# A convolution kernel whose GpSimd pieces and VectorE sums are put in another order, and whose pieces are held behind an earlier VectorE instruction

## The chip, the cores and the metric

The kernel runs on one core of a Trainium2 chip. The core's engines are TensorE (PE, matrix products; its weight loads are listed as PEld), VectorE (DVE), ScalarE (ACT), GpSimd (POOL) and SyncE (SP, which here only issues DMAs). Each engine works through its own queue in order, and engines wait for each other on semaphores. The metric is the device time of one execution in microseconds (us): the median of three runs of the kernel before is 270.39 us (270.06 to 271.07).

## The reference

A gated causal convolution over time with three taps, two steps apart, followed by a projection:

```python
B, T, D, K, dil = 2, 16000, 256, 3, 2
h = sum over i of  xp[:, pad - 2*i : pad - 2*i + T] @ w[i]     # w[i]: 256 x 512, pad = 4
f, g = h[..., :D], h[..., D:]
z = tanh(f) * sigmoid(g)
return z @ w_o                                                  # w_o: 256 x 256
```

Inputs and the output are bf16.

## The kernel before

**Fast convolution.** Time steps are laid out as rows of J neighbouring steps (`xt`, transposed on load, 128 channels on the partitions). For J = 4 (a B group) four products of 512 columns, each in two contraction steps, give two pairs of output steps in place of six products; for J = 6 (an A group) five products give three pairs. The price is linear combinations of the input ("input sums") ahead of the products, and linear combinations of the results behind them.

**Input sums.** For a B group: `m`, `p`, `d0`, `d3`. For an A group: `u0`, `u1`, `u2`, `e`, `f`, three scalings of `u1` (`u3`, `uh`, `ud`), and four sums on top of others: `rp` = f + u1 and `rm` = e + u3, made by an accumulating DMA that POOL issues, and `r0` = u0 + uh and `ri` = u2 + ud. Sums of 128x1024 elements are VectorE's (`pre`, L434 for two inputs, L432 for a scaling). `r0`, `ri` and, from group 5 on, `d0` and `d3` are GpSimd's, each in four quarters of 128x256, called pieces. Sixteen pieces `wa` (L351) build a weight for the A groups at the start. The trace names `r0` by the tile `u`, `d0` and `d3` by `d`.

**Blocks and slots.** There are 12 A groups and 13 B groups with four blocks each (one 128-wide part of the 512 outputs), 100 blocks in all: first 16 B blocks, then A and B mixed 48 to 28, then 8 B blocks. The main loop takes one block per turn `k`, called slot k here. In slot k TensorE makes the "first" product of block k (and "mid" for an A block), "last" of block k - 1, "zero" and "inf" of block k - 2 (`product`, L453), and one or two output pieces of the projection (`out_mm`, L565). So `m` or `u1` is due in a group's first slot, `p` and `rp` one later, `d0`, `d3`, `r0` and `ri` two later, `rm` in the first slot's "mid". ScalarE copies the first product out (`ss`), applies tanh and sigmoid, and evicts the projection.

**VectorE's order in a slot.** A gate (tanh times sigmoid, L547; 128x1024 for B, 128x1536 for A, every other slot of a group, and for one small remainder `zo`, L543), then a *combine* (L487, reading PSUM) of block k - 1, a second one for an A block, and `halfway` (L487) for block k if that is an A block. All L487 operations are called combines here; they are the only ones that read PSUM. Between them stand the input sums, at *stops*: each gate and each first combine calls `at_stop`, which takes the next line of the string `PLAN`. Of a line "`a > b ; c`", `b` are sums that VectorE makes at this stop, `c` pieces and DMAs that go to POOL's queue, and `a` are sums made at the end of the slot (`ahead`).

**Holds.** A piece is issued with a wait (`hold`) for an earlier VectorE instruction, the `latest` one that `note` has recorded: the last sum of the stop, or, without sums, the gate or combine before it. So pieces start when the stop's combine starts. The two kinds of DMA have no such wait; POOL issues them in its order once their inputs are there.

```python
def at_stop():
    sums(stop[1])
    gpsimd(stop[2])
    stop = next(stops, [[], [], []])
```

**Loads.** SP issues the transposing load of a group (L286) at the end of the slot 15 ahead of its `wanted` slot; an A or a B group's tile has four buffers.

Of the kernel before, what the change touches and what calls it, by code (L numbers as in the profile page):

```python
# [117 lines left out]
>uh.9;ri.9
>u3.9 p.9;r0.9 d3.9 d3.9
>f.9;  # L120
>;rm.9 d0.9
# [16 lines left out]
>f.11;d3.10
>u2.11;rp.11 d3.10 d3.10
>uh.11;  # L140
>;rm.11 d3.11 d0.11
>ud.11 u0.11;r0.11 d3.11 ri.11 d3.12
>;ri.11 d0.12 r0.11 r0.11 ri.11
# [33 lines left out]
def kernel(  # L177
# [10 lines left out]
    nc = tc.nc  # L188
# [3 lines left out]
    K, _, D2 = w.shape  # L192
# [148 lines left out]
    def weights_a(n):  # L341

        if n < 2 * K:
            tap, ct = n % K, n // K
            nc.scalar.mul(wu_sb[tap][ct][:], w_taps[tap][:, ct, :], (-2.0 / 3.0, -1.0 / 3.0, -1.0 / 6.0)[tap])
            return None
        n -= 2 * K
        add, ct, part = n // (2 * W_A), n // W_A % 2, n % W_A
        d = slice(part * D2 // W_A // 16 * 16, (part + 1) * D2 // W_A // 16 * 16)
        dst = (wu_sb[0][ct], wa_sb[:, ct, :])[add]  # L350
        return nc.gpsimd.tensor_tensor(out=dst[:, d], in0=wu_sb[0][ct][:, d], in1=wu_sb[1 + add][ct][:, d], op=ALU.add)  # L351
# [65 lines left out]
    def pre(g, name, eng, qs=slice(0, 4), behind=None):  # L417
        G = groups[g]
        R = G["R"]
        op, factor, a, b = operand(g, name)  # L420
        if name not in G:
            if name in ON_TOP:

                G[name] = G[ON_TOP[name]]
            else:
                pool = {"m": pre_pool, "p": pre_pool, "u3": sum_pool, "uh": sum_pool, "ud": sum_pool, "d0": dif_pool, "d3": dif_pool}.get(name, dif_pool)
                G[name] = pool.tile([P, 2, CT, RG], bf16, name=name, tag=name)
        if name in BY_DMA:
            return nc.gpsimd.dma_start(out=G[name][:, :, :, :R], in_=b, accum_op=op)
        o, a, b = (t if t is None else t.rearrange("p q ct r -> p (q ct) r")[:, qs] for t in (G[name][:, :, :, :R], a, b))  # L430
        if op is None:
            ins = eng.tensor_scalar_mul(o, a, factor)  # L432
        else:
            ins = eng.tensor_tensor(out=o, in0=a, in1=b, op=op)  # L434
        return hold(ins, behind)
# [97 lines left out]
    def gate(g, dt):  # L533
        at_stop()
        G = groups[g]
        R, J = G["R"], G["J"]
        n = R // P * P
        if "z" not in G:
            G["z"] = z_pool.tile([P, NT, J, RG], bf16, name="zz", tag=f"zz{J}")
            if n < R:  # L540
                G["zo"] = z_pool.tile([P, NT, J * (R - n)], bf16, name="zo", tag="zo")
        if n < R:
            nc.vector.tensor_tensor(  # L543
                out=G["zo"][:, dt, :].rearrange("p (j r) -> p j r", j=J), in0=G["th", dt][:, :, n:R],
                in1=G["sg", dt][:, :, n:R], op=ALU.mult,
            )
        note(nc.vector.tensor_tensor(  # L547
            out=G["z"][:, dt, :, :n], in0=G["th", dt][:, :, :n], in1=G["sg", dt][:, :, :n], op=ALU.mult
        ))
# [50 lines left out]

    kinds = {n: groups[g]["kind"] for n, (g, _) in enumerate(seq)}
    stops = iter([[part.split() for part in re.split("[>;]", line)] for line in PLAN.strip().split("\n")])
    stop = next(stops)
    latest, quarters = [None], {}

    def note(ins):
        latest[0] = ins
        return ins  # L610
# [27 lines left out]
    def at_stop():  # L638
        nonlocal stop
# [44 lines left out]
    while k < N + 3 or todo or made:  # L684
        b0, b1, b2, b3 = (seq[n] if 0 <= n < N else None for n in (k, k - 1, k - 2, k - 3))
        kind = groups[b0[0]]["kind"] if b0 else None
        n = 1 + (len(todo) >= SOME_A) if kind == "A" else (k >= N + 3) + (not b0 or len(todo) >= SOME) + 1
# [46 lines left out]
        if b3 and b3[1] in (1, 3):  # L734
            g, dt = b3[0], b3[1] // 2
# [53 lines left out]
```

## Time and profile before

| What | Value |
|---|---|
| Median of three runs | 270.39 us |
| The profiled execution, in all | 271.02 us |
| Its span, first to last instruction | 269.2 us |
| Granted TensorE clock | 1.00 |
| PE, DVE, ACT, POOL busy, share of the span | 97%, 90%, 91%, 49% |
| Pieces: `r0`, `ri` (`u<-u,uh` and `u<-u,ud`), 48 each | 671 and 696 ns mean |
| Pieces: `d0`, `d3` (`d<-xt`), 64 in all | 618 ns mean |
| Accumulating DMAs `rp` (`f<-u`), `rm` (`e<-u`), 12 each | 5.1 and 3.8 us to land |

A line of a timeline gives start, duration, engine, line, operation, output<-input and shape, and in brackets the idle time of the engine before it with what ended it. Durations on VectorE overlap a little: the next instruction starts some 0.09 us before the recorded end of the one before (combines of 0.68 follow each other every 0.60, a two-input sum of 0.69 takes 0.61, a scaling of 0.42 takes 0.34). A wait for several semaphores is put down to the last. A profile describes one execution.

### The profile page before, as it was taken

Reading aid. Unit: us, or ns where it says so; the run is one execution under the profiler, and the core shown is the slowest. Engines: PE = TensorE matmul, PEld = TensorE weight load, DVE = VectorE, ACT = ScalarE, POOL = GpSimd, SP = SyncE. Lnnn points to the kernel's source line nnn. Section 1 sums busy time; section 2 is a strip of 40 time slices with the busy share of each in tenths; the row PEclk is TensorE's granted clock in tenths of the full one; section 3 lists DMA queues with packets and bytes.
Section 4 is the critical chain, followed back from the end, with each engine's and each line's share of the span. In section 5 each row is a group of like instructions: output and inputs, shape, how many; then the busy total and the mean of one; then the engine's idle time right before and its main releaser. Section 6 shows DMA issues by size and latency. Waiting matters only on the chain.

```text
span 269.2 us, 4529 instructions
## 1 busy us (share of the span) xinstructions
PE 262.4 (97%) x1476; PEld 143.7 (53%) x1476; DVE 243.6 (90%) x396; ACT 246.2 (91%) x487; POOL 130.7 (49%) x209
## 2 busy tenths in 40 slices
PE   8999999999999999999999999999999999999993
PEld 5644555454555555555555555555555555555682
DVE  2899999999999999999999999999999897797372
ACT  5799999889999999989989998999999999999983
POOL 1024333787565564657645274464446668514000
PEclk9999999999999999999999999999999999999999
DMA  7999998559772699329658786691627764121225
GB/s 196 222 158 226 233 185 214 145 103 199 105 183 98 120 242 249 97 98 230 173 130 206 166 177 123 138 264 65 138 107 143 149 153 119 59 78 60 100 97 185
DMA packets 79583, 41.25 MB, mean 153 GB/s; under 512 B 68648, under 2 KB 69928, under 8 KB 79560
## 3 DMA queue, kind: packets, MB, share of 16 engines
q1 hardware_dynamic: 75060, 33.66, 51.2%
q0 software_dynamic: 3456, 6.29, 14.6%
q10 hardware_dynamic: 1044, 1.02, 1.2%
q8 instruction: 11, 0.18, 0.3%
q14 instruction: 12, 0.10, 0.1%
HBM read 1.25 MB, written 16.38 MB: 65 GB/s over the span
## 4 chain that ended last, share of the span: by engine, by line
PE 88%; DVE 8%; POOL 1%; issue 1%; ACT 0%; DVEq 0%
PE b L453 51%; PE o_ps L565 19%; PE a L453 14%; DVE a L487 2%; PE b L473 2%; DVE zz L547 2%; DVE yy L487 1%; DVE hh L487 1%; PE a L473 1%; PE a L268 1%; POOL u L434 1%; DVE f L434 1%; PE fill L300 0%; DVE e L434 0%; PE tp L360 0%
## 5 line engine op out<-in xcount | busy, mean ns | idle before, releaser
L487 DVE SCALAR_TENSOR_TENSOR a<-ss,b 128x512 f32<-128x512 f32 (+1 forms) x100 | 68.0, 680 | 9.3 <-PE b L453 8.7
L592 ACT CAST osb<-o_ps 128x512 bf16<-128x512 f32 x118 | 70.6, 598 | 5.0 <-PE o_ps L565 4.7
L565 PE MATMUL o_ps<-wo_sb,zz 128*128 128x256 bf16 x496 | 69.9, 273 | 0.0
L453 PEld LDWEIGHTS <-w_sb 128*128 128x128 bf16 x400 | 38.7, 97 | 48.3 <-DVE yy L487 2.9
L484 ACT COPY ss<-b 128x512 f32<-128x512 f32 (+1 forms) x100 | 59.8, 598 | 3.5 <-PE b L453 1.3
L565 PEld LDWEIGHTS <-zz 128*128 128x128 bf16 x496 | 48.5, 98 | 25.3
L434 POOL TENSOR_TENSOR d<-xt 128x256 bf16<-128x256 bf16 (+1 forms) x64 | 38.8, 618 | 39.8 <-DVE m L434 10.9
L434 POOL TENSOR_TENSOR u<-u,ud 128x256 bf16<-128x256 bf16 x48 | 33.1, 696 | 25.3 <-DVE zz L547 8.3
L434 POOL TENSOR_TENSOR u<-u,uh 128x256 bf16<-128x256 bf16 x48 | 31.9, 671 | 27.2 <-DVE zz L547 10.5
L547 DVE TENSOR_TENSOR zz<-th,sg 128x1024 bf16<-128x1024 bf16 (+2 forms) x52 | 42.7, 821 | 1.9 <-ACT sg L527 1.5
L487 DVE SCALAR_TENSOR_TENSOR hh<-ss,b 128x512 f32<-128x512 f32 x48 | 32.6, 680 | 3.2 <-PE b L453 2.9
L527 ACT ACTIVATE th<-a 128x512 bf16<-128x512 f32 (+1 forms) x50 | 30.5, 611 | 2.9 <-PE a L453 2.4
L453 PEld LDWEIGHTS <-wp_sb 128*128 128x128 bf16 x200 | 19.4, 97 | 25.3 <-issue 4.9
L487 DVE SCALAR_TENSOR_TENSOR yy<-hh,b 128x512 f32<-128x512 f32 x48 | 32.5, 678 | 0.0
L527 ACT ACTIVATE sg<-a 128x512 bf16<-128x512 f32 (+1 forms) x50 | 30.7, 614 | 1.7 <-PE a L453 0.9
L527 ACT ACTIVATE th<-b 128x512 bf16<-128x512 f32 (+1 forms) x50 | 30.5, 609 | 0.6 <-PE b L453 0.6
L527 ACT ACTIVATE sg<-b 128x512 bf16<-128x512 f32 (+1 forms) x50 | 30.6, 611 | 0.4 <-PE b L453 0.4
L453 PE MATMUL b<-d,w_sb 128*128 128x512 bf16 (+1 forms) x104 | 30.3, 372 | 0.3 <-DVE a L487 0.2
L453 PE MATMUL a<-d,w_sb 128*128 128x512 bf16 (+1 forms) x104 | 30.3, 373 | 0.0
L453 PE MATMUL b<-m,wm_sb 128*128 128x512 bf16 (+1 forms) x104 | 30.3, 373 | 0.0
L453 PE MATMUL b<-p,wp_sb 128*128 128x512 bf16 (+1 forms) x104 | 30.3, 373 | 0.0
L453 PE MATMUL b<-u,w_sb 128*128 128x512 bf16 x96 | 28.6, 379 | 0.6 <-DVE yy L487 0.5
(57 smaller groups left out, 333.7 us busy)
## 6 DMA issues: line engine op xcount, KB each, us to landing
out_dram<-osb SPq DMA_DIRECT2D x24, 384.0 KB, 2.9
out_dram<-osb SPq DMA_DIRECT2D x26, 256.0 KB, 2.6
f<-u POOLq DMA_DIRECT2D x12, 256.0 KB, 5.1
e<-u POOLq DMA_DIRECT2D x12, 256.0 KB, 3.8
w_sb<-in_w_dram ACTq DMA_DIRECT2D x3, 256.0 KB, 4.0
xt<-in_x_dram SPq DMA_TRANSPOSE x25, 5.5
xn<-in_x_dram SPq DMA_DIRECT2D x1, 160.0 KB
xn<-in_x_dram ACTq DMA_DIRECT2D x1, 160.0 KB, 4.3
```

The source lines that it names most:

```text
L268: nc.tensor.matmul(wps[:], lhsT=ones[:, 0:P], rhs=ones, start=True, stop=True,)
L434: ins = eng.tensor_tensor(out=o, in0=a, in1=b, op=op)
L453: nc.tensor.matmul(G[bank, oi][:, :2 * R], lhsT=wmat[:, ct, osl], rhs=G[mv][:, :, ct, :R], start=which == "first" and ct == 0, stop=ct == ...
L473: nc.tensor.matmul(G[bank, oi][:, :4 * r].rearrange("p (j r) -> p j r", j=4), lhsT=w_taps[tap][:, ct, osl], rhs=xt[:, j0:j0 + 4, ct, c0 + ...
L484: nc.scalar.copy(out=G["ss", oi][:, :n], in_=G["b", oi][:, :n])
L487: return note(nc.vector.scalar_tensor_tensor(out=out, in0=in0, scalar=scalar, in1=in1, op0=ALU.mult, op1=op))
L527: nc.scalar.activation(out=G[name, dt][:, j:j + 2, :R], in_=G[bank, oi][:, :2 * R].rearrange("p (q r) -> p q r", q=2), func=(ACT.Tanh, ACT ...
L547: note(nc.vector.tensor_tensor(out=G["z"][:, dt, :, :n], in0=G["th", dt][:, :, :n], in1=G["sg", dt][:, :, :n], op=ALU.mult))
L565: nc.tensor.matmul(o_ps[:, q, :], lhsT=z, rhs=wo_sb[:, dt, :], start=dt == 0 and (q == 0 or len(dts) == NT), stop=dt == NT - 1, skip_group ...
L592: copy(out=osb[:, 2 * jp:2 * jp + 2, :], in_=o_ps[:])
```

## The change

`PLAN` is another list: the same sums, pieces and DMAs at other stops, and in another order within many. The first eight-and-twenty lines before and after, and the last ones:

```diff
@@ -12,152 +12,152 @@
 PLAN = """
->d0.0 m.0 d3.0 p.0;
->d0.1;wa.0
->m.1;
->;wa.1
->p.1 d3.1 m.2;wa.8
->;
->d0.2;wa.7 wa.2 wa.5
->u1.0 uh.0;wa.6
->p.2;
->;wa.4
->d3.2 e.0;wa.9
->m.3 f.0;
->;wa.12 wa.10
->u3.0 u1.1 u0.0;r0.0
->uh.1;
->u2.0;wa.3
->u0.1 p.3;
->d0.3 d3.3;
->;rp.0 wa.15
->m.4 e.1;rm.0 wa.14
->u2.1;
->d3.4;wa.11 r0.0
->ud.1 u3.1 u1.2;r0.0
->u3.2 p.4;
->ud.0;ri.1
->d0.4 f.1;rm.1 ri.0 r0.0 ri.0
->;
->uh.2;wa.13 ri.0 ri.0
...
+>m.0 p.0 d3.0 d0.0;
+>d3.1;wa.2
+>m.1;
+>;wa.1
+>p.1 d0.2 m.2;wa.5' wa.7
+>d0.1;
+>;wa.0
+>e.0 u1.0;wa.10
+>p.2;
+>;wa.8 wa.9
+>d3.2 f.0;wa.6' wa.13'
+>m.3;
+>ud.0;wa.4' wa.12
+>uh.0 u0.0 u0.1;r0.0''
+>u2.0;
+>u3.0;ri.0'
+>u2.1 d0.3;wa.14' wa.3
+>d3.3;
+>p.3;rp.0 r0.0'
+>p.4 f.1;wa.11'
+>u0.2;
+>u1.1;rm.0 r0.0'
+>d0.4 m.4;ri.0' d0.5'
+>u1.2;
+>d3.4;r0.0'
+>ud.1 uh.2 e.1 uh.1;rp.1 r0.2' wa.15
+>;
+>u3.1;r0.2' ri.0 ri.0
...
+>m.12 p.11;d3.11' d0.11
...
+p.12>;d0.12
...
@@ -540,10 +540,10 @@
             if n < R:
                 G["zo"] = z_pool.tile([P, NT, J * (R - n)], bf16, name="zo", tag="zo")
         if n < R:
-            nc.vector.tensor_tensor(
+            note(nc.vector.tensor_tensor(
                 out=G["zo"][:, dt, :].rearrange("p (j r) -> p j r", j=J), in0=G["th", dt][:, :, n:R],
                 in1=G["sg", dt][:, :, n:R], op=ALU.mult,
-            )
+            ))
         note(nc.vector.tensor_tensor(
             out=G["z"][:, dt, :, :n], in0=G["th", dt][:, :, :n], in1=G["sg", dt][:, :, :n], op=ALU.mult
         ))
@@ -600,13 +600,14 @@
 
 
 
+
     kinds = {n: groups[g]["kind"] for n, (g, _) in enumerate(seq)}
     stops = iter([[part.split() for part in re.split("[>;]", line)] for line in PLAN.strip().split("\n")])
     stop = next(stops)
-    latest, quarters = [None], {}
+    made_v, quarters = [], {}
 
     def note(ins):
-        latest[0] = ins
+        made_v.append(ins)
         return ins
 
     def group_of(token):
@@ -619,9 +620,10 @@
 
     def gpsimd(tokens):
         for token in tokens:
-            token, _, n = token.partition("x")
+            behind = made_v[-1 - token.count("'")]
+            token, _, n = token.strip("'").partition("x")
             if token.startswith("wa"):
-                hold(weights_a(2 * K + int(token[3:])), latest[0])
+                hold(weights_a(2 * K + int(token[3:])), behind)
                 continue
             g, name = group_of(token)
             if name in BY_DMA:
@@ -629,7 +631,7 @@
                 continue
             had = quarters.get((g, name), 0)
             quarters[g, name] = had + int(n or 1)
-            pre(g, name, nc.gpsimd, slice(had, quarters[g, name]), behind=latest[0])
+            pre(g, name, nc.gpsimd, slice(had, quarters[g, name]), behind=behind)
 
     def ahead():
         sums(stop[0])
```

A token may now end in one or two primes. A piece without a prime is held as before behind the last recorded VectorE instruction, with one prime behind the one before it, with two behind the one before that. `note` keeps all recorded instructions in a list, and the gate's small remainder is recorded too. Primes stand only at stops with sums. Slots that the prediction speaks of, in VectorE's order (G gate; C, Y, H the combines; POOL's tokens in square brackets, where they stand in the program):

| Slot | Before | After |
|---|---|---|
| 3 | p.1 d3.1 m.2 [wa.8] C | p.1 d0.2 m.2 [wa.5' wa.7] C |
| 7 | d3.2 e.0 [wa.9] C | d3.2 f.0 [wa.6' wa.13'] C |
| 15 | ud.1 u3.1 u1.2 [r0.0] C | d0.4 m.4 [ri.0' d0.5'] C |
| 18 | G uh.2 [wa.13 ri.0 ri.0] C Y H | G u3.1 [r0.2' ri.0 ri.0] C Y H |
| 20 | e.2 f.2 [rp.1 d3.5 r0.1 d0.5 ri.1] C H | f.2 e.2 [rm.1 ri.1' r0.1 r0.1'] C H |
| 24 | G [ri.2 ri.1 ri.1] C Y H | G [ri.1 d3.5 ri.1 ri.2 d3.5] C Y H |
| 29 | u3.3 f.3 [r0.3 ri.2 d0.6] C Y H | u1.4 u3.4 [rp.3 d0.6 d0.6'' ri.2' d3.6''] C Y H |
| 38 | G u2.4 [r0.4 r0.4] C Y | G u1.5 [rm.4 d3.7'] C Y |
| 39 | uh.5 u0.5 ud.4 [d3.6 r0.4] C H | u2.4 uh.5 m.7 [r0.4' ri.4''] C H |
| 48 | ud.6 p.7 [d0.7 d0.8 ri.5] C Y H | f.6 u2.6 [rm.6 r0.6'' ri.5 r0.5 d0.7] C Y H |
| 56 | G [r0.6 d3.8] C Y H | G [ri.7 d0.8 d0.8 ri.7] C Y H |
| 59 | G [rp.7 r0.7 r0.7 d3.9] C Y H | uh.7 G [r0.7 d0.9 r0.7 d3.8] C Y H |
| 66 | G e.9 [d3.9 ri.8] C H | f.9 G u3.9 [ri.8' r0.8 r0.8] C H |
| 85 | ud.11 u0.11 [r0.11 d3.11 ri.11 d3.12] C H | [ri.11 ri.11] C H |
| 86 | [ri.11 d0.12 r0.11 r0.11 ri.11] C Y H | [r0.11 r0.11] C Y H |
| 87 | G [r0.11 d3.12 ri.11] C Y | m.11 G [r0.11 d0.11] C Y |
| 92 | p.12 [d0.11 d0.11] C Y | m.12 p.11 [d3.11' d0.11] C Y |
| 96 | G C | G C p.12 |

Batches of pieces in slots 3 to 69, by the number of pieces (DMAs not counted) and of combines directly behind the stop; "primed" batches begin with a piece that has a prime:

| Pieces, combines | Before | After, no prime | After, primed |
|---|---|---|---|
| 1, 1 | 10 | 2 | 6 |
| 1, 2 | 12 | 6 | 6 |
| 2, 1 | 2 | 1 | 5 |
| 2, 2 | 21 | 3 | 21 |
| 2, 3 | 6 | 5 | 3 |
| 3, 1 | 1 | 0 | 0 |
| 3, 2 | 4 | 0 | 2 |
| 3, 3 | 8 | 0 | 1 |
| 4, 2 | 1 | 0 | 0 |
| 4, 3 | 0 | 3 | 1 |
| 5, 3 | 0 | 1 | 0 |
| all | 65 | 21 | 45 |

More of the change, by code (lines that the diff above doesn't have):

```diff
@@ L116 @@
->e.10;ri.8 r0.8
->;
[L118 to L121, printed above, removed]
->;
->;d0.9
->u0.10 u1.11 uh.10;rp.9 ri.9 r0.9
->u3.10 f.10;r0.9 ri.9
+>p.1 d0.2 m.2;wa.5' wa.7
[20 more added lines that the diff above has]
+>ud.1 uh.2 e.1 uh.1;rp.1 r0.2' wa.15
+>;
@@ new lines @@
+>u3.1;r0.2' ri.0 ri.0
+>m.5 u3.2;d3.5'
+>f.2 e.2;rm.1 ri.1' r0.1 r0.1'
+>;
+>;r0.2 r0.1
+>;
+>u1.3;ri.1' d0.5'
+>u2.2 ud.2;d0.5' r0.1
+>;
+>;ri.1 d3.5 ri.1 ri.2 d3.5
+>e.3;
+>p.5 u3.3 f.3;rm.2 ri.2' d3.5'
+>ud.3;
+>;rp.2 r0.2
+>;
+>uh.3;d0.5' d3.6'
+>u1.4 u3.4;rp.3 d0.6 d0.6'' ri.2' d3.6''
+>u0.3;ri.2
+>;
+>u2.3;r0.3' d3.6
+>f.4 uh.4;rm.3 ri.3' r0.3''
+>;
+>u0.4;ri.3' d0.6
+>;
+>e.4;r0.3' r0.3
+>ud.4 m.6;d0.6' r0.4'
+>p.6 e.5;ri.3' ri.3''
+>;
+>;d3.6 r0.4
+>;
+>u1.5;rm.4 d3.7'
+>u2.4 uh.5 m.7;r0.4' ri.4''
@@ new lines @@
+>;
+>;rp.4 d3.7 r0.4
+>e.6 u3.5 ud.5;ri.4' ri.4
+>u0.5 f.5;r0.5' ri.4''
+>;
+>;r0.5 d3.7
+>;
+>u1.6;rp.5 d0.7
+>p.7 u2.5;rm.5 d3.7'
+>ud.6;
+>uh.6;ri.5' r0.5'
+>u3.6 u0.6;ri.5' d0.7'
+>f.6 u2.6;rm.6 r0.6'' ri.5 r0.5 d0.7
+>;
+>;ri.5
+>;
+>f.7;rp.6 d0.7' r0.6'
+>u1.7;ri.6' r0.6'
+>u0.7 u2.7;ri.6' ri.6
+>;
+>u3.7;r0.6' ri.6
+>m.8 ud.7 e.7;d0.8' d3.8''
+>u1.8;
+>;rm.7 d3.8
+>;
+>;ri.7 d0.8 d0.8 ri.7
+>p.8;d0.8'
+>e.8 u3.8 u0.8;rp.7 ri.7' d3.8''
+>uh.7;
+>;r0.7 d0.9 r0.7 d3.8
+>;
+>;ri.7
+>f.8 u2.8;d3.9' d0.9''
@@ L126 @@
+>;
+>;r0.7 r0.7
+>uh.8 e.9 ud.8;rm.8 ri.8''
+>u1.9 uh.9;rp.8 d3.9 ri.8''
+>;
+>ud.9;ri.8'
+>f.9;
+>u3.9;ri.8' r0.8 r0.8
+>u2.9;ri.9' r0.8'
+>u0.9;d0.9 r0.8
+>m.9;
+>;d3.9 d3.10
+>u1.10;rm.9 r0.9
+>;
+>p.9;rp.9 r0.9' d3.9'
+>;
+>uh.10;d0.9' d0.10'
+>f.10 e.10;r0.9 ri.9''
+>u3.10 u1.11;d0.10 ri.9''
 >;
@@ L128 @@
 >;
->m.10;d0.10 r0.10
->u3.11 ud.10 u2.10;rm.10 rp.10
+>u2.10;rm.10 d0.10' d3.10
+>u3.11 u0.10 ud.10;rp.10 ri.10'
 >;
 >;r0.10 ri.10 r0.10
->p.10;ri.10 ri.10 d0.10
->e.11;d0.10 d0.10
+>ud.11 p.10;r0.10' r0.10''
+>e.11 m.10;d3.11' d3.11''
 >;
->;ri.10 r0.10 d3.10
+>;ri.10 d3.10 ri.10
 >;
[L138 to L143, printed above, removed]
->;
->;r0.11 d3.12 ri.11
->;
->;
->;d3.11
->m.11 p.11;
->;
->m.12;d3.11 d0.12 d3.12 d3.12
->p.12;d0.11 d0.11
+>;d0.10 d0.11
+>f.11 uh.11 u2.11;rm.11 d3.10 d3.12'
+>u0.11;
+>;rp.11 ri.11 r0.11 d3.12 ri.11
+>;ri.11 ri.11
+>;r0.11 r0.11
+>m.11;
+>;r0.11 d0.11
+>;
+>;
+>;d3.11 d0.12 d3.12 d0.12
+>;d0.12
 >;
 >;d0.11
+>m.12 p.11;d3.11' d0.11
+>;
+>;d3.12
 >;
 >;
->;d0.12
 >;
 >;
->;d0.12
+>;
+p.12>;d0.12
 >;
```

57 lines of the change are left out of this document (removed).

## The prediction

> **What bounds the kernel now.** The page comes first: TensorE (PE) looks like the bound.
>
> ```profile
> PE 262.4 (97%) x1476; PEld 143.7 (53%) x1476; DVE 243.6 (90%) x396; ACT 246.2 (91%) x487; POOL 130.7 (49%) x209
> ```
>
> A mean hides stages, so the second view is the busy time by stage: 16.5 to 66.5 (slots 3 to 24), 66.5 to 184 (slots 25 to 69), and the rest.
>
> ```profile
> 16.50:66.50 50.00, 49.49 (x261) 25.15 (x259) 49.82 (x82) 46.14 (x90) 25.70 (x41) 1.00 0.88 184
> 66.50:184.00 117.50, 117.20 (x643) 62.35 (x641) 116.54 (x190) 111.45 (x220) 66.78 (x102) 1.00 0.74 165
> 184.00:262.00 78.00, 77.54 (x459) 44.67 (x457) 64.63 (x105) 74.58 (x150) 36.51 (x57) 1.00 0.38 104
> ```
>
> The columns are length, PE, PEld, DVE, ACT, POOL. VectorE (DVE) is busy 166.4 of 167.5 us in the first two stages and only 64.6 of 78 in the third. From slot 3 to slot 69 VectorE sets the pace as much as TensorE; after that TensorE alone does. DVE's waits between 16.5 and 184 say the same: two, 0.4 us in all.
>
> ```profile
> DVE zz L547 <- ACT sg L527: 0.2, 1, 0.2
> DVE hh L487 <- PE o_ps L565: 0.2, 1, 0.2
> ```
>
> What PE loses is read from where slots begin (first matmul of a block) against PE's own pace, which the chain in order of time gives: 2.16 us for a slot with four product pairs, 2.60 with five.
>
> ```profile
> 16.75 1.29 PE b L453 x6
> 18.91 1.29 PE b L453 x6
> ...
> 202.31 1.29 PE b L453 x6
> 204.90 1.29 PE b L453 x6
> 207.50 1.34 PE b L453 x6
> ```
>
> ```profile
> 18.75 0.59 PE L453 MATMUL b<-m,wm_sb 128*128 128x512 bf16 x2
> ...
> 64.41 0.59 PE L453 MATMUL b<-u,wa_sb 128*128 128x512 bf16 x2
> ...
> 181.30 0.59 PE L453 MATMUL b<-u,wa_sb 128*128 128x512 bf16 x2
> ```
>
> Slots 4 to 23 take 64.41 - 18.75 = 45.66. Their pace is 14 x 2.16 + 2 x 1.73 (slots 5 and 6 have no output piece) + 4 x 2.60 = 44.1, so 1.5 us is lost. Slots 24 to 68 take 116.9 against 38 x 2.60 + 7 x 2.16 = 113.9: 3.0 lost. One more loss, 0.5 us, is a late GpSimd (POOL) piece at 232.85. So at most 5.0 us can be won.
>
> What slows VectorE is its neighbour:
>
> ```profile
> 41.84 0.46 POOL L351 TENSOR_TENSOR wa_sb<-wu,wu 128x128 bf16<-128x128 f32 x1 [2.12 <-DVE d L434]
> 42.21 0.42 DVE L432 TENSOR_SCALAR ud<-u 128x1024 bf16<-128x1024 bf16 x1
> 42.26 0.90 POOL L434 TENSOR_TENSOR u<-u,uh 128x256 bf16<-128x256 bf16 x1
> 42.55 0.90 DVE L432 TENSOR_SCALAR u<-u 128x1024 bf16<-128x1024 bf16 x1
> ```
>
> The piece at 42.26 met a running sum, which kept its 0.42; the piece took 0.90 instead of 0.67 and ended 0.53 after that sum. The sum at 42.55 took 0.90 instead of 0.42, ending 0.28 after the piece. An SBUF sum and a piece exclude each other, first come first served; combines, which read PSUM, run beside pieces at 0.68 in any case. A clean tensor_tensor sum is 0.686, a scaling 0.415, a gate 0.683 or 0.952. Means by form between 16.5 and 184 show the surplus: uh 613 x10 (2.0 us), u3 548 x9 (1.2), ud 479 x10 (0.6), u 710 x31 (0.8), gates 732 x17 and 969 x16 (1.1), f 0.2: 5.9 us, of which 2.4 lie before 66.5.
>
> **The change, part by part.** The same sums, pieces and DMAs are issued; no operation is added or removed, and the extra note on the gate's remainder adds no instruction.
>
> *Holds.* Before, a batch of pieces is held behind the last sum of its stop. It starts 0.08 to 0.23 after that sum's end (44.13 after 44.04), while the combine began 0.08 before the end. With a pitch of 0.60 per combine and 0.625 per piece, n pieces under n combines overrun by about 0.1, and the next sum pays it, as at 47.14:
>
> ```profile
> 46.70 0.67 POOL L434 TENSOR_TENSOR u<-u,ud 128x256 bf16<-128x256 bf16 x1 [1.91 <-DVE ud L432]
> 47.14 0.78 DVE L434 TENSOR_TENSOR d<-xt 128x1024 bf16<-128x1024 bf16 x1
> ```
>
> Held one instruction earlier, the piece arrives about 0.17 after the sum's start, is shut out, and ends 0.53 after the sum's end as at 42.26. That is as long as the combine leaves, whose 0.60 began 0.08 before that end, and the next sum needs the port only 0.13 after its start (it ends 0.55 after a piece, of 0.686). Each further combine has room for a further piece. In slots 3 to 69 the before order has 65 batches: 10 of one piece under one combine and 29 of n under n = 2 or 3 (0.1 each, 3.9 us if all reach a sum), and 8 with more pieces than combines (the row of 42.55: 0.48 each, 3.8). That is 7.7 against 5.9 measured: the count is a ceiling. After: 66 batches, 45 of which begin with a piece held one or two instructions earlier. Of these 28 have n = combines and cost nothing; 5 batches held the old way cost 0.1 each. Thirteen have more pieces than combines: five of the short weight pieces (0.45), in slots 3 to 11, take 0.3 together; slots 15, 20, 48 and 66 have an SBUF sum or gate straight behind them, 0.48 each, 1.9; in slots 24, 29, 56 and 59 the sum gets in between two pieces, 0.1 each. Sum 3.1, of which 1.5 before slot 24. VectorE gets back 5.9 - 3.1 = 2.8 us, 0.9 of it by slot 24. The bounds are 0, if the early hold gains nothing, and 5.9.
>
> One sentence on a rule: the Trainium skill's "SBUF — State Buffer", section "SBUF: two separate sides", says that the shared port pair is an exclusive lock and that "the other fully blocks". By it a shut-out piece would need its whole 0.67 from the sum's end, not 0.53 as traced; n under n would still fit (0.67 against 0.60 plus 0.13 of a sum's lead-in), the overfull batches would cost 0.14 more each, and the time would be some 0.4 us longer; the row is used.
>
> *Order.* Sums at 0.606 (tensor_tensor) and 0.335 (scaling) of pitch: through slot 24 before has 36 and 9 (24.8 us), after 37 and 9 (25.4), so 0.6 more lies early; through slot 69 after has 0.3 less.
>
> *(a) Slots 4 to 23:* VectorE -0.9 + 0.6 = -0.3, and VectorE is the pace here: PE loses 1.2 in place of 1.5. Bounds +0.6 (order alone) and -1.5.
>
> *(b) Slots 24 to 68:* VectorE -1.9 - 0.9 = -2.8 of the 3.0 that PE loses. Not all arrives, for PE is late next on other things: the collisions behind slots 48 and 66 fall in one slot each, which has no more than 0.3 to spare (0.2 each, 0.4); slot 68 took 2.34 in place of 2.16, its end released by a ScalarE activation, not VectorE, and two more short slots are likely to do so (0.15 each, 0.3); and a load. Slot 38 now has a piece d3.7 and slot 39 the sum m.7, while the block's transpose, second of two that SP issues from 90.86 to 100.1, landed at 103.5, after slot 39 began at 102.54. POOL waits some 2 us with r0.4 and ri.4 behind it (due in slot 44), and m.7 meets the late piece: 0.4. So -2.8 + 1.1 = -1.7. Bounds 0 and -3.0. The loads first used in slots 69, 80 and 83 land within 1 us of use; VectorE has spare time there, price 0.
>
> *(c) Slots 69 to the end:* the stall at 232.85 goes, since all pieces of the last six-row group but one are placed by slot 86, before in slots 85 to 87: -0.5. The sum p.11 moves to slot 92, one before its use, and p.12 behind the combine of slot 96: +0.1 for both, hidden by VectorE's waits of 2 us there. Net -0.4; bounds +0.3 and -0.5.
>
> The start is even: four sums ahead of the first gate either way. The scratch-weight pieces change order and stay before slot 17, their first use. Accumulating DMAs (0.87 to issue, 3.8 to 5.1 to land) have at least 3 slots, before 2.
>
> Sum: -0.3 - 1.7 - 0.4 = -2.4 us. The profiled execution was 271.02 (span 269.2 and 1.8 around it), so 268.6 on its scale; it lies 0.6 above the median 270.39. On the median: **268.0**.
>
> **Rivals.** *Same:* VectorE is freed but TensorE and ScalarE do not follow. ACT is busy 111.45 of 117.5; if each of the seven short slots then costs 0.3 and the four collisions 0.4 each, (b) shrinks to nothing and (a) to noise: about 269.8. For it: 95% ACT; against: slots 70 to 86 ran at 2.60 with ACT no less loaded. The case that the early holds do nothing, because POOL is behind anyway, ends here too, at 270.4 by order alone.
>
> *Slower:* the early piece gets there before VectorE's last sum has begun to read. The sum then ends 0.08 + 0.67 + 0.55 after the hold instead of 0.60, 0.7 late. Over 45 batches that is 31 us; it decides from six batches on (4.2 against 2.4 gained and 1.35 that can be told apart), and 12 batches, 8.4 - 2.4, give 276.4. Against: the sum starts 0.09 before its forerunner's recorded end and the piece at least 0.08 after it; at 42.26, 0.05 of lead was enough for the sum. For: at 228.97 a gate with a piece 0.02 behind it lost. [...]
>
> ```profile
> 228.97 1.24 DVE L547 TENSOR_TENSOR zz<-th,sg 128x1024 bf16<-128x1024 bf16 x1
> 228.99 0.67 POOL L434 TENSOR_TENSOR u<-u,ud 128x256 bf16<-128x256 bf16 x1
> ```
>
> *Much faster:* no loss remains in slots 4 to 86: 270.4 - 5.0 = 265.4.
>
> **Chances.** Forecast (266.5 to 269.0) 0.55, much faster 0.10, same 0.20, slower 0.15. Half a per cent, 1.35 us, is about what a measurement here can tell: faster 0.65, same 0.20, slower 0.15. The range runs from 265.9 to 271.2, leaving out most of the slower case and the last bit of the much faster one; the forecast's own is 266.5 to 269.0.
>
> **What would show it.** Right: DVE's means by form between slots 3 and 69 fall (uh, u3 and ud towards 0.42, gates to 0.68 and 0.95), pieces run longer (0.9 to 1.1) because they wait inside, DVE idles some us before slot 69, slots 24 to 68 take about 115.3, and the stall at 232.85 is gone. Wrong: sums of 1.2 us and more behind many batches (slower), or clean sums with ACT as releaser of PE's waits (same). A late m.7 near slot 39 would show as DVE waiting for a DMA.

## The result and the profile after

Four runs of the kernel after gave a median of 267.94 us (267.66 to 268.64), beside 270.63 of the kernel before: a ratio of 0.9906 (95% interval 0.9878 to 0.9934). Two later comparisons, each with runs of the kernel before on the same chip, gave 0.9903 (0.9889 to 0.9918) and 0.9918 (0.9906 to 0.9931). The change saves 2.2 to 2.7 us; 2.4 were forecast.

The same views as before, of the profiled execution after (267.66 us, span 265.8). First the engine line of the page, then the stages (length, PE, PEld, DVE, ACT, POOL, clock, DMA share, GB/s), and VectorE's waits in the first two stages:

```profile
PE 259.5 (98%) x1476; PEld 143.0 (54%) x1476; DVE 240.0 (90%) x396; ACT 245.9 (92%) x487; POOL 144.2 (54%) x209
```

```profile
16.50:66.50 50.00, 49.78 (x261) 25.12 (x260) 49.70 (x84) 46.37 (x90) 31.19 (x44) 1.00 0.94 192
66.50:184.00 117.50, 117.23 (x652) 63.56 (x651) 114.89 (x190) 112.52 (x223) 78.08 (x105) 1.00 0.73 164
```

```profile
DVE a L487 <- PE b L453: 0.8, 3, 0.3
DVE zz L547 <- ACT sg L527: 0.5, 3, 0.2
DVE hh L487 <- PE b L453: 0.2, 1, 0.2
DVE hh L487 <- ACT th L527: 0.2, 1, 0.2
```

VectorE's work is 3.6 us shorter and POOL's 13.5 longer, though both execute the same instructions: VectorE waits far less inside its sums, and the pieces wait inside theirs. VectorE's waits between instructions have grown from 0.4 to 1.7 us, and they are for TensorE and ScalarE. Between 66.5 and 184 it is busy 114.89 of 117.5. The groups of VectorE by form between 16.5 and 184 show where its time came from, first three of the kernel before, then those of the kernel after:

```profile
L547 DVE TENSOR_TENSOR zz<-th,sg 128x1024 bf16<-128x1024 bf16 x17 | 12.4, 732 | 0.1
L432 DVE TENSOR_SCALAR uh<-u 128x1024 bf16<-128x1024 bf16 x10 | 6.1, 613 | 0.1
L432 DVE TENSOR_SCALAR u<-u 128x1024 bf16<-128x1024 bf16 x9 | 4.9, 548 | 0.0
```

```profile
L547 DVE TENSOR_TENSOR zz<-th,sg 128x1536 bf16<-128x1536 bf16 x16 | 15.3, 954 | 0.5 <-ACT sg L527 0.5
L547 DVE TENSOR_TENSOR zz<-th,sg 128x1024 bf16<-128x1024 bf16 x17 | 11.8, 695 | 0.0
L432 DVE TENSOR_SCALAR uh<-u 128x1024 bf16<-128x1024 bf16 x10 | 4.5, 446 | 0.1
L432 DVE TENSOR_SCALAR u<-u 128x1024 bf16<-128x1024 bf16 x10 | 4.2, 421 | 0.0
L432 DVE TENSOR_SCALAR ud<-u 128x1024 bf16<-128x1024 bf16 x10 | 4.2, 420 | 0.0
```

The scalings are down to 0.42 to 0.45 (`u<-u` is u3), the gates to 0.695 and 0.954. How a primed piece does it is read from slots 16 and 18 in the timeline:

```profile
44.60 0.68 DVE L434 TENSOR_TENSOR d<-xt 128x1024 bf16<-128x1024 bf16 x1
44.75 1.06 POOL L434 TENSOR_TENSOR u<-u,uh 128x256 bf16<-128x256 bf16 x1 [1.23 <-DVE zz L547]
...
45.80 0.41 DVE L432 TENSOR_SCALAR ud<-u 128x1024 bf16<-128x1024 bf16 x1
...
49.24 0.42 DVE L432 TENSOR_SCALAR u<-u 128x1024 bf16<-128x1024 bf16 x1
49.40 0.78 POOL L434 TENSOR_TENSOR u<-u,uh 128x256 bf16<-128x256 bf16 x1 [0.93 <-DVE zz L547]
...
50.14 1.30 POOL L434 TENSOR_TENSOR u<-u,ud 128x256 bf16<-128x256 bf16 x2
...
51.36 0.69 DVE L434 TENSOR_TENSOR m<-xt 128x1024 bf16<-128x1024 bf16 x1
```

The piece at 44.75 comes 0.15 after the start of the last sum, is shut out, and ends at 45.81, 0.53 after that sum's end. The next sum begins at 45.80 and takes its clean 0.41. In slot 18 three pieces end at 51.44, and the sum that begins at 51.36 is clean too: the 0.08 fall into its first 0.13, in which it does not need the port.

The late piece at the end is gone. In the kernel before, TensorE stood still for 0.50 in the middle of a pair of products, until the piece that it reads had ended at 232.79:

```profile
231.32 1.47 POOL L434 TENSOR_TENSOR u<-u,ud 128x256 bf16<-128x256 bf16 x1
...
232.14 0.38 PE L453 MATMUL a<-u,w_sb 128*128 128x512 bf16 x1
...
232.85 0.38 PE L453 MATMUL a<-u,w_sb 128*128 128x512 bf16 x1 [0.34 <-POOL u L434]
```

In the kernel after, the same pair runs without a gap:

```profile
229.28 0.59 PE L453 MATMUL a<-u,w_sb 128*128 128x512 bf16 x2
```

The slots from which the stages are measured begin here, in PE's timeline (slots 4, 24 and 69):

```profile
17.80 0.38 PE L453 MATMUL b<-m,wm_sb 128*128 128x512 bf16 x1
...
62.84 0.38 PE L453 MATMUL b<-u,wa_sb 128*128 128x512 bf16 x1
...
178.44 0.38 PE L453 MATMUL b<-u,wa_sb 128*128 128x512 bf16 x1
```

The table gives these stages, from the start of one slot to that of the next named, for one profiled execution of each kernel; the experiments of the next section stand in it too (after_again and after_third are the kernel after once more, timed beside other kernels). "Excess" is VectorE's time in slots 3 to 69 above the clean durations (0.688, 0.418, gates 0.685 and 0.953); the last columns count the sums and gates of those slots with an excess of over 0.30 us and of 0.05 to 0.15.

| Kernel | Median, us | Slot 4 begins | 4 to 23 | 24 to 68 | 69 to 92 | 93 to the end | Excess | > 0.30 | 0.05 to 0.15 |
|---|---|---|---|---|---|---|---|---|---|
| before | 270.33 | 18.75 | 45.67 | 116.89 | 62.65 | 25.28 | 5.7 | 6 | 14 |
| after | 267.94 | 17.80 | 45.04 | 115.59 | 62.16 | 25.23 | 2.0 | 2 | 6 |
| after_again | 267.88 | 17.78 | 45.23 | 115.59 | 62.17 | 25.26 | 2.0 | 2 | 6 |
| order_only | 269.24 | 18.76 | 46.06 | 115.50 | 62.16 | 25.25 | 4.6 | 1 | 23 |
| holds_only | 269.44 | 17.70 | 45.38 | 116.32 | 62.67 | 25.25 | 3.9 | 5 | 6 |
| before_nopieces | 267.66 | 17.70 | 45.00 | 115.20 | 62.17 | 25.27 | 0.6 | 0 | 2 |
| after_nopieces | 268.02 | 17.67 | 46.87 | 115.19 | 62.16 | 25.25 | 0.7 | 0 | 2 |
| one_earlier | 282.25 | 18.05 | 49.76 | 123.85 | 63.25 | 25.50 | 17.5 | 34 | 7 |
| stall_only | 269.75 | 17.93 | 45.67 | 116.93 | 62.16 | 25.24 | 5.8 | 6 | 14 |
| after_third | 267.96 | 18.02 | 46.41 | 115.56 | 62.15 | 25.27 | 1.6 | 2 | 6 |
| one_prime | 267.80 | 18.20 | 45.03 | 115.15 | 62.15 | 25.25 | 1.0 | 1 | 5 |
| better | 267.89 | 18.67 | 45.04 | 115.16 | 62.16 | 25.27 | 1.3 | 1 | 5 |
| better_again | 267.47 | 18.08 | 45.05 | 115.15 | 62.15 | 25.25 | 1.1 | 1 | 5 |
| swap | 267.53 | 18.27 | 45.02 | 115.14 | 62.15 | 25.28 | 1.5 | 1 | 5 |

From slot 4 on the kernel after is 0.63 + 1.30 + 0.49 + 0.05 = 2.47 us shorter. That it also began slot 4 0.95 earlier in its profile need not be the change's work; the last section shows why.

### The profile page after: what moved, and what is told of

Same layout as the page of the kernel before. It is cut to its first block, busy times and chain, and to the rows that moved or that the text cites. A ratio compares the mean times of both kernels' runs of the same rounds, so it can differ in the third digit from the quotient of the medians.

```text
span 265.8 us, 4535 instructions
## 1 busy us (share of the span) xinstructions
PE 259.5 (98%) x1476; PEld 143.0 (54%) x1476; DVE 240.0 (90%) x396; ACT 245.9 (92%) x487; POOL 144.2 (54%) x209
## 3 DMA queue, kind: packets, MB, share of 16 engines
q10 hardware_dynamic: 1044, 1.02, 1.2%
## 4 chain that ended last, share of the span: by engine, by line
PE 87%; DMA 3%; ACT 3%; DVE 3%; SPq 1%; issue 1%; DVEq 0%
PE b L453 52%; PE o_ps L565 20%; PE a L453 15%; DMA xt<-in_x_dram 2%; DMA w_sb<-in_w_dram 1%; ACT th L527 1%; ACT ss L484 1%; DVE a L487 1%; SPq L286 1%; DVE yy L487 1%; ACT sg L527 1%; DVE hh L487 1%; ACT osb L592 0%; DVE zz L547 0%; DVE p L434 0%
## 5 line engine op out<-in xcount | busy, mean ns | idle before, releaser
L434 POOL TENSOR_TENSOR d<-xt 128x256 bf16<-128x256 bf16 (+1 forms) x64 | 41.9, 663 | 35.2 <-DVE zz L547 11.3
L434 POOL TENSOR_TENSOR u<-u,uh 128x256 bf16<-128x256 bf16 x48 | 37.6, 789 | 24.9 <-DVE zz L547 17.3
L434 POOL TENSOR_TENSOR u<-u,ud 128x256 bf16<-128x256 bf16 x48 | 36.9, 775 | 24.5 <-DVE zz L547 12.9
L547 DVE TENSOR_TENSOR zz<-th,sg 128x1024 bf16<-128x1024 bf16 (+2 forms) x52 | 41.4, 796 | 2.1 <-ACT sg L527 2.1
```

What stands on the lines that cost most here:

```text
L547: note(nc.vector.tensor_tensor(out=G["z"][:, dt, :, :n], in0=G["th", dt][:, :, :n], in1=G["sg", dt][:, :, :n], op=ALU.mult))
```

## The experiments

**Order and holds apart.** *order_only* is the kernel after with every prime ignored, so all pieces are held the old way; *holds_only* is the kernel before with its old list and one prime, in effect, on each piece of a stop with sums:

```diff
 order_only
-            behind = made_v[-1 - token.count("'")]
+            behind = made_v[-1]
 holds_only
-    def gpsimd(tokens):
+    def gpsimd(tokens, early):
+        behind = made_v[-1 - early]
...
-        gpsimd(stop[2])
+        gpsimd(stop[2], len(stop[1]) > 0)
```

> The new list of stops, but every piece held behind the last VectorE instruction, as before the change (primes ignored). Theory (the earlier hold is what frees VectorE): 33 batches with as many pieces as combines overrun by 0.1 us again and the overfull ones by about 0.5, so VectorE's surplus between slots 3 and 69 goes back from 2.4 to 5 to 6.5 us, and the time is 269.5 to 271. Rival (the order, with fewer pieces in a row, is what helps): the surplus stays at 2 to 3 us and the time within 0.7 us of 268.0.

> The old list of stops, but at every stop with sums the pieces are held behind the instruction ahead of the last sum. Theory (earlier hold): the overrun of 0.1 us in 39 batches goes, the 8 overfull batches keep about 0.5 each, VectorE's surplus falls from 5.9 to about 3 us and the time to 268.0 to 269.0, with the late piece near 230 us still costing 0.5. Rival (order): 270 to 271, no change against the kernel before.

Measured: order_only 269.24 (269.14 to 269.52), ratio 0.9955 (0.9939 to 0.997); holds_only 269.44 (269.1 to 270.15), ratio 0.9971 (0.996 to 0.9982); the kernel after, on the same chip, 267.88 (267.8 to 268.01). Neither part was worth what the theory of the holds alone expected: the order gives 1.1 us and was to give nearly nothing, the holds 0.9 and were to give most. Their sum, 2.0, is close to the 2.45 of both.

The stages tell more than the totals. The order alone takes slots 24 to 68 from 116.89 to 115.50 (115.59 with both) and removes the stall of the last part; in slots 4 to 23 it costs 0.39 us, as it brings 0.6 us of sums forward there. The holds repair just that: with both, these slots take 45.04. In slots 24 to 68 the holds lower the excess further, from 2.05 to 1.1 us, and the time does not move, but two effects cancel there: the kernel after has one misplaced piece in slot 48 that costs 0.44, and without it (one_prime, below) these slots take 115.15. On the new order the holds are thus worth 0.35 us in these slots. The two last columns say why so little. The groups of order_only between 16.5 and 184:

```profile
L547 DVE TENSOR_TENSOR zz<-th,sg 128x1024 bf16<-128x1024 bf16 x17 | 12.6, 741 | 0.0
L434 DVE TENSOR_TENSOR m<-xt 128x1024 bf16<-128x1024 bf16 x8 | 6.1, 759 | 0.0
L434 DVE TENSOR_TENSOR d<-xt 128x1024 bf16<-128x1024 bf16 x7 | 5.2, 743 | 0.0
L432 DVE TENSOR_SCALAR uh<-u 128x1024 bf16<-128x1024 bf16 x10 | 4.2, 418 | 0.1
```

The scaling uh, which lost 0.2 us on average, is clean without any early hold, and m, d and the gates lose some 0.06 each instead. The new order took away five of the six large collisions (over 0.30 us); it left, and added, small ones of about 0.1, and seven of 0.22 to 0.30, five of them in slots 4 to 12. The early holds take away small ones (14 to 6 on the old order) and leave five large ones, four of them where they were. Slots 24 to 68 show what the size of a collision means: holds_only has 2.28 us of excess there, with three large collisions, and takes 1.12 us longer than the kernel without pieces (below); order_only has 2.05, with none over 0.26, and takes 0.30 longer. That a large one is felt because a late combine holds up TensorE, while small ones vanish in what the slots have to spare, fits these figures but was not tested one collision at a time. In slots 4 to 23 more of the excess reaches the time: from order_only to the kernel after it falls by 1.6 us, and the slots are 1.02 shorter.

**No pieces.** From before and after the pieces of r0, ri, d0 and d3 were left out; the products read u0, u2 and the loaded rows in their place, so the output is not the reference's:

```diff
             g, name = group_of(token)
...
+            if name in ON_TOP:
+                groups[g][name] = groups[g][ON_TOP[name]]
+            continue
```

(The DMAs `rp` and `rm` stay: they are issued in the lines left out. The products take the loaded rows where `d0` or `d3` does not exist.)

> The old list and holds, with every piece of r0, ri, d0 and d3 left out (their products read u0, u2 or the loaded rows instead), so the result is not the reference's; the sixteen weight pieces and the DMAs stay. Theory (contention between pieces and sums is what the change relieves): with none left the old order runs at least as fast as the changed kernel, 266.6 to 267.8. Rival (the order of the sums): without contention the old order still keeps most of its losses, 269 or more.

> The kernel after with GpSimd's pieces of r0, ri, d0 and d3 left out (the products read u0, u2 and the loaded rows instead, so what is computed is not the reference). If the order is worth something only because it places pieces, this takes the same time as the kernel before without its pieces: 267.2 to 268.0, and it is at most 0.7 below the kernel after, whose remaining contention would then be worth that little. If the order of the sums itself were worth the 1.1 us that the order alone gave, it would take 266.0 to 266.6. VectorE's means by form should be clean in either case.

Measured: before_nopieces 267.66 (267.08 to 268.93), ratio 0.9901 (0.9868 to 0.9934); after_nopieces 268.02 (267.97 to 268.94), ratio 0.9906 (0.9886 to 0.9925). Slots 24 to 68 take 115.20 and 115.19, so the order is worth nothing there if no piece stands in VectorE's way. Slots 4 to 23 take 45.00 and, less a wait of 1.94 us for a load that the profile of after_nopieces shows in slot 3 (below), 44.93. All that these pieces cost the kernel before is therefore 0.67 + 1.69 + 0.48 = 2.84 us, and the kernel after has won back all but 0.4 of it (115.59 against 115.20). The 0.6 us of excess that remain are contention too: most of it lies in slots 4 to 9, where the weight pieces `wa` still run. In before_nopieces a sum that begins at 28.26 takes 0.95 in place of 0.69 beside two weight pieces (27.55 to 28.65), and the same sum takes 0.95 in the kernel before. The pieces of r0, ri, d0 and d3 thus make 5.1 us of the excess of before, and 1.4 of that of after.

**One instruction earlier still.** Each primed piece of the kernel after was given one more prime:

```diff
-            behind = made_v[-1 - token.count("'")]
+            behind = made_v[-1 - token.count("'") - ("'" in token)]
```

> The kernel after, with every primed piece held one VectorE instruction earlier still, so that it arrives beside the last instruction but one ahead of the combine and not beside the last. Lock theory (a shared port, first come first served): the piece gets in between two SBUF operations and the later one waits for it, 0.47 us each time, as in slot 48 of the kernel after, where a doubly primed r0.6 stretched u2.6 from 0.69 to 1.16. Some 39 batches of slots 3 to 69 meet two SBUF operations in a row (22 two sums, 17 a gate and a sum), so VectorE grows by up to 18 us, 2.6 of which its waits take: 278 to 283 us, with tensor_tensor sums of 1.1 to 1.2 us by the dozen. The rival, that it matters only that a piece comes early and not beside which instruction, gives 268 to 269 and sums of unchanged length.

Measured: 282.25 (282.02 to 282.43), ratio 1.0432 (1.0414 to 1.045), excess 17.5 us against some 18 expected, 34 sums and gates with over 0.30. The rival, for which it only matters that a piece comes early, is out. One of the 34 in the timeline of one_earlier:

```profile
49.46 0.68 DVE L434 TENSOR_TENSOR e<-xt 128x1024 bf16<-128x1024 bf16 x1
49.63 1.04 POOL L434 TENSOR_TENSOR u<-u,uh 128x256 bf16<-128x256 bf16 x1 [1.09 <-DVE uh L432]
50.07 0.89 DVE L432 TENSOR_SCALAR uh<-u 128x1024 bf16<-128x1024 bf16 x1
50.88 0.68 DVE L487 SCALAR_TENSOR_TENSOR a<-ss,b 128x512 f32<-128x512 f32 x1
```

The piece is behind e and ahead of uh in the row for the port: it ends 0.53 after e, and uh ends 0.29 after the piece, at 0.89 in place of 0.42. This is the mechanism of the slower rival of the prediction, at 0.41 to 0.48 a batch in all but one of the 34 cases (the prediction had put 0.7), and it shows how narrow the useful place is: one instruction later costs 0.1, one earlier 0.47.

**Slot 48.** The trace after has one such case of its own. There r0.6 carries two primes, and f.6 and u2.6 are two sums in a row:

```profile
124.63 0.69 DVE L434 TENSOR_TENSOR f<-xt 128x1024 bf16<-128x1024 bf16 x1
124.87 0.98 POOL L434 TENSOR_TENSOR u<-u,uh 128x256 bf16<-128x256 bf16 x1
125.23 1.16 DVE L434 TENSOR_TENSOR u<-xt 128x1024 bf16<-128x1024 bf16 x1
...
127.64 0.59 PE L453 MATMUL b<-u,w_sb 128*128 128x512 bf16 x2 [0.26 <-DVE yy L487]
```

TensorE then loses 0.43 and 0.17 us on two combines in a row (pairs of products that begin 0.86 and 0.60 after the one before, where 0.43 is usual). *one_prime* takes one prime away; *better* does that, hands d0.7 on to slot 49 and ri.2 and d3.5 of slot 24 to slot 25, and takes one prime from r0.0 in slot 9:

```diff
 one_prime
->f.6 u2.6;rm.6 r0.6'' ri.5 r0.5 d0.7
+>f.6 u2.6;rm.6 r0.6' ri.5 r0.5 d0.7
 better
->f.6 u2.6;rm.6 r0.6'' ri.5 r0.5 d0.7
->;
->;ri.5
+>f.6 u2.6;rm.6 r0.6' ri.5 r0.5
+>;
+>;ri.5 d0.7
...
->;ri.1 d3.5 ri.1 ri.2 d3.5
->e.3;
+>;ri.1 d3.5 ri.1
+>e.3;ri.2' d3.5'
...
->uh.0 u0.0 u0.1;r0.0''
+>uh.0 u0.0 u0.1;r0.0'
```

> The kernel after with three of its crowded stops thinned: slot 48 has r0.6 with one prime in place of two and hands d0.7 to slot 49; slot 24 hands ri.2 and d3.5 to slot 25, there held behind the instruction ahead of the sum; r0.0 in slot 9 has one prime in place of two. TensorE lost 0.43 and 0.17 behind slot 48 and 0.25 and 0.16 behind slot 24. If these were the collisions' doing, 0.6 to 1.0 us less than the kernel after (267.9): 266.9 to 267.3. If VectorE no longer sets the pace there and ScalarE takes over, within 0.2 of the kernel after. The loss behind slot 24 stands in all kernels so far (0.42 to 0.49), pieces late or early, so it is the doubtful one: 0.6 is the likelier gain.

> The kernel after, for comparison with the two below on one chip: 267.9, as twice before; slots 24 to 68 at 115.59.

> The kernel after with one character gone: r0.6 in slot 48 has one prime in place of two, and still has three pieces behind it in the slot. If TensorE's 0.60 us behind slot 48 is the work of the piece that gets in ahead of u2.6 (1.16 us in place of 0.69), then u2.6 is clean, the slot's surplus moves to the gate of slot 49 (up to 0.48, four pieces under three combines), and 0.35 to 0.5 of the loss is gone, since the order alone (all of the slot's pieces behind u2.6) lost 0.12 there: slots 24 to 68 at 115.1 to 115.25, the time at 267.4 to 267.6. If the number of pieces in the slot is what costs, the loss stays and only moves to the gate: 267.9.

> The version with slots 9, 24 and 48 thinned, again. Its stages were 45.04, 115.16 and 62.16 against 45.04, 115.59 and 62.16 of the kernel after, but slot 4 began at 18.67 in place of 17.80, and the time came out the same. If the start differs by chance alone, five rounds beside the kernel after on the same chip show the stage's gain: 0.3 to 0.5 less than the kernel after, 267.4 to 267.6. If thinner stops earlier in the program delay the start, it stays at 267.9.

Measured: in the first comparison better took 267.89 (267.37 to 268.12), ratio 0.9898 (0.9882 to 0.9915), no less than the kernel after had taken; in the second the kernel after (after_third) 267.96 (267.72 to 269.42), one_prime 267.80 (267.42 to 268.64), better (better_again) 267.47 (267.08 to 267.98), ratio 0.9903 (0.9891 to 0.9916). Between the kernel after and these two the totals alone decide little; the stage does. Slots 24 to 68 took 115.56 to 115.59 in three profiles of the kernel after and 115.14 to 115.16 in four without the second prime, whatever else was thinned, and one_prime alone has the whole 0.44. Its slot 48:

```profile
125.00 0.69 DVE L434 TENSOR_TENSOR f<-xt 128x1024 bf16<-128x1024 bf16 x1
...
125.61 0.68 DVE L434 TENSOR_TENSOR u<-xt 128x1024 bf16<-128x1024 bf16 x1
...
125.87 0.95 POOL L434 TENSOR_TENSOR u<-u,uh 128x256 bf16<-128x256 bf16 x1 [0.40 <-DVE f L434]
...
128.00 0.68 DVE L547 TENSOR_TENSOR zz<-th,sg 128x1024 bf16<-128x1024 bf16 x1
128.04 1.12 POOL L434 TENSOR_TENSOR d<-xt 128x256 bf16<-128x256 bf16 x1
```

The expected 0.48 at the gate did not come: the fourth piece started 0.04 after the gate and was the one to wait. So it was the place of one piece, not the number of pieces in the slot. With 115.15 these slots have reached the time without pieces (115.20), so placing the pieces otherwise has nothing left to gain in them. The loss of 0.25 and 0.16 behind slot 24 stands in better_again as before, and without pieces too: it was the doubtful one of the expectation, and it is not the pieces'; what causes it was not tried.

**The stall alone.** In the kernel before only, the pieces of slots 85 to 87 were put in another order:

```diff
->ud.11 u0.11;r0.11 d3.11 ri.11 d3.12
->;ri.11 d0.12 r0.11 r0.11 ri.11
+>ud.11 u0.11;r0.11 ri.11 r0.11 ri.11
+>;ri.11 r0.11 r0.11 ri.11 d3.11
 >;
->;r0.11 d3.12 ri.11
+>;d0.12 d3.12 d3.12
```

> The kernel before with one edit at its end: in slots 85 to 87 the eight pieces of r0 and ri of the last six-row group stand ahead of the pieces of d0 and d3 that are due six and more slots later; all else, holds too, is as before. If the wait of TensorE for the late piece (0.50 us at 232.85) is simply added to the end, 0.45 to 0.55 us less: 269.8, and slots 69 to 92 at 62.15 in place of 62.65. If TensorE only catches up there with work that is late for another reason (ScalarE, the loads), nothing changes: 270.3.

Measured: 269.75 (269.53 to 270.06), ratio 0.9971 (0.9959 to 0.9983). Slots 69 to 92 take 62.16 in place of 62.65, exactly what the kernel after takes there, and the second piece-fed pair runs without a gap (PE's timeline of stall_only):

```profile
228.77 0.59 PE L453 MATMUL a<-u,w_sb 128*128 128x512 bf16 x2
...
231.37 0.59 PE L453 MATMUL a<-u,w_sb 128*128 128x512 bf16 x2
```

The stall is added to the end in full, and all of stage (c) is this stall.

**A load in slot 3.** The profile of after_third has 46.41 us in slots 4 to 23, 1.4 more than the others. Its VectorE timeline in slot 3:

```profile
15.80 0.69 DVE L434 TENSOR_TENSOR p<-xt 128x1024 bf16<-128x1024 bf16 x1
17.88 0.70 DVE L434 TENSOR_TENSOR d<-xt 128x1024 bf16<-128x1024 bf16 x1 [1.39 <-DMA xt<-in_x_dram]
```

This is d0.2, the first to use the load of group B2. The change moved it ahead of m.2, so the load is used 0.60 us earlier than before, when d3.1 stood there. Where VectorE waited for it in slot 3, the wait ended at 16.43, 16.59, 16.71, 17.88 and 18.08; the kernel before would have come to it at 17.73. *swap* is better with the two sums exchanged:

```diff
->p.1 d0.2 m.2;wa.5' wa.7
->d0.1;
+>p.1 d0.1 m.2;wa.5' wa.7
+>d0.2;
```

> The version with slots 9, 24 and 48 thinned, and the sums d0.1 (slot 4) and d0.2 (slot 3) exchanged, so that the load of group B2 is first used by m.2, 0.60 us later, as in the kernel before. In four profiles of kernels of the new order VectorE waited 0.04, 0.19, 1.39 and 1.94 us in slot 3 for that load, which landed between 16.8 and 18.9 as SP's entries show it. If these waits are part of what spreads the runs, each gets up to 0.6 shorter: the median at 267.1 to 267.5 (267.47 without the exchange), no run above 268.3, and in the profile no wait ahead of d0.2. If the start alone spreads them, nothing changes: 267.4 to 267.9 with runs up to 268.7.

Measured: 267.53 (267.25 to 267.93), ratio 0.99 (0.9881 to 0.9919), no run above 267.93, and no wait in slot 3; but in this profile d0.1 began at 16.66 and m.2 at 17.26, and the load was there by then, so the exchange spared 0.6 at most and was hardly put to the test. (SP's entries, by which the expectation dated the load, are no good measure: in better d0.2 began without a wait at 17.05, while the entry ended at 18.40.) That the wait makes some runs longer is shown by two profiles (268.94 of after_nopieces and 269.2 of after_third, against medians of 268.02 and 267.96); that the exchange cures it is not shown.

Three measurements of the thinned list (0.9898 and 0.9903, and 0.99 with the two sums exchanged) lie at or below three of the kernel after (0.9903, 0.9906, 0.9918), with overlapping intervals. Its stage from slot 24 to 68 is 0.44 us shorter in every profile, but no total proves that the whole is faster.

## Why the prediction was right, and where it was not

*What bounds the kernel.* Right. Collisions of sums and pieces made VectorE late, VectorE held TensorE from slot 3 to 69, and the kernel without pieces is as fast as the kernel after.

*The holds: n pieces under n combines, the first one shut out by the last sum, cost nothing.* Right, as slots 16 and 18 show. One instruction earlier costs some 0.47 (34 cases), by the slower rival's mechanism; wherever the sum or gate was 0.1 to 0.35 us ahead, in all 14 profiles, it came first.

*What is left of the excess (3.1 us, 1.5 of it before slot 24).* Too high: by the same groups it is 2.4, and 0.9 of that are there without the pieces of r0, ri, d0 and d3, mostly beside the weight pieces. Of the four overfull batches at 0.48 each, slot 15 cost 0.34, slots 20 and 66 under 0.1, and slot 48 0.47, but by its second prime, not by its length. The step that failed is "have an SBUF sum or gate straight behind them, 0.48 each": it took the piece to win against what follows, and in slots 20, 48 (once mended) and 66 it did not.

*That the holds are what relieves VectorE, and the order only moves sums.* Wrong in part, and the sum came out in part by luck. The holds did relieve VectorE the more (on the new order its excess falls from 4.6 to 2.0 us, while the order alone takes it from 5.7 to 4.6), but the time followed the order as much. The price of the order was put at +0.6 by slot 24 and -0.3 by slot 69, for the work of its sums alone. In fact it took away five of six large collisions by itself and gave 1.39 us in slots 24 to 68; the holds would have added 0.35 there, and the second prime of slot 48 took that back. The count of batches by pieces and combines did not see this: it gives the new order held the old way some 33 batches at 0.1 and 13 at 0.48, 9.5 us, and 4.6 were measured. The number of pieces alone does not decide; which instruction follows a batch, and when it comes, was left out of the count.

*(a), -0.3 forecast, -0.63 measured.* The two terms as such were good: +0.39 by order alone, for +0.6, and the holds -1.02 (46.06 to 45.04), for -0.9. The 0.3 between forecast and result are these two differences, 0.21 and 0.12.

*(b), -1.7 forecast (-2.8 + 1.1), -1.30 measured.* VectorE's excess fell by 2.2 there, not 1.9; the 0.9 of sums moved stand as counted from the list. Of the deductions, behind slots 48 and 66 0.4 were taken and 0.44 lost, all in slot 48; ScalarE's 0.3 was too much, for TensorE's loss on its account rose by less than 0.1 (0.33 to 0.41); and the late load of m.7, 0.4, did not happen: SP issued it at 93.0 and not at 96.1, as its entry for the load ahead began 1.6 earlier and took 3.7 us in place of 5.2, and it was there at 97.6, before slot 38 began. The step that failed is the size of the prize, "-2.8 of the 3.0 that PE loses". The 3.0 are right (by the pitch of its matmuls, 0.216 each, TensorE loses 3.1 there, 2.8 released by VectorE and 0.3 by ScalarE), but the kernel without pieces shows that only 1.69 of them are the pieces'. The other 1.4 stay with clean sums; what would lift them was not tried. That -1.30 came near -1.7 is thus partly luck: a prize counted 1.1 too high met deductions of 1.1 of which 0.4 came true.

*(c), -0.4 forecast, -0.49 measured.* The stall went, as stall_only shows by itself; the 0.1 for p.11 and p.12 did not appear.

*The start, even.* As far as the order goes, yes; what it did not name is the load that slot 3 now meets 0.60 sooner.

*Rivals.* Same: ScalarE did not take over. Much faster: 265.4 counted on 5.0 us, and 2.84 exist. Slower: the mechanism is real but needs one instruction more of lead, and in the kernel after it is seen in slot 48. The Trainium skill's page "SBUF — State Buffer", section "SBUF: two separate sides", has the shared port as a lock that the first one keeps for its whole instruction; the traces agree on who comes first where one is 0.1 us or more ahead (for nearer ties see the last section), and keep to the measured 0.53 (44.75 to 45.81 behind a sum that ended at 45.28) where "fully blocks" would give 0.67.

## What to carry to other kernels

Where two engines exclude each other on a port, have the less urgent one arrive just after the last long instruction of the other has begun, and count its place in instructions: one too late cost 0.1 us here, one too early 0.47. Before costing such a change, measure a kernel without the contending work: its stages give the whole prize (2.84 us here, not the 5.0 that TensorE lost against its pace) and show where nothing is left. Here a few large collisions cost the engine downstream far more than many small ones of the same sum, so look for the large ones first, and compare by stages from a late common point, since the start varies.

## What the runs showed that was not expected

**The start varies by a microsecond, whatever the list.** Slot 4 began between 17.67 and 18.76 in 14 profiles, at 18.75 and 17.93 in two kernels that are the same up to slot 84 (before and stall_only), and at 18.67 and 18.08 in two profiles of one kernel (better and better_again); so the three early starts of the kernel after (17.80, 17.78, 18.02) need not be the change's work. Most of the difference lies in the direct products of the first steps (L473), eighteen matmuls that took 3.35 to 3.49 us in the three profiles with a start after 18.6 and 2.62 to 2.83 in the others. PE's timeline of before, and then of after:

```profile
5.11 3.44 PE L473 MATMUL b<-xt,w_sb 128*128 128x320 bf16 x18
```

```profile
4.90 2.62 PE L473 MATMUL b<-xt,w_sb 128*128 128x320 bf16 x18 [0.16 <-ACT xt L365]
```

In the three late profiles the first six or seven of these matmuls begin 0.27 us apart and the rest 0.14; in the others two at most are spaced like that. TensorE thus runs at half its pace at first, and the moment at which this ends differs from one execution to the next, although the recorded clock is 1.00 in these stretches too. What sets that moment, no run here shows. An early start is partly lost again, as VectorE then runs into the loads of slots 1 to 3: it waited 0.2 to 2.4 us for them in ten of the eleven profiles that began slot 4 before 18.3, and not at all in the three after 18.6.

**Who wins a tie.** A gate that began 0.02 ahead of a piece lost to it in the kernel before (228.97, 1.24 in place of 0.68), and the same gate lost with 0.035 in holds_only. Yet a gate that began 0.04 ahead won (128.00 in one_prime), and so did one that began together with its piece in the kernel before:

```profile
231.32 1.47 POOL L434 TENSOR_TENSOR u<-u,ud 128x256 bf16<-128x256 bf16 x1
231.33 0.94 DVE L547 TENSOR_TENSOR zz<-th,sg 128x1536 bf16<-128x1536 bf16 x1
```

In the 14 profiles all seventeen sums and gates that began within 0.015 us of a piece won. The recorded starts are therefore not the moments at which the port is taken, and for leads below some 0.04 us they do not tell who gets it.
